# Attention with a gated feed-forward on one core: the first batch in one piece, with two of its head groups paired

## The chip, the cores and the metric

The kernel runs on one core of a Trainium2 chip. The metric is the device time of one execution in microseconds (us). A core has five engines with instruction queues of their own: TensorE (PE in the profile; its weight loads are PEld), VectorE (DVE), ScalarE (ACT), GpSimd (POOL) and SyncE (SP). They meet through semaphores only. Here POOL's queue issues all loads, and SP's (with a few on ACT's) issues all stores.

## The reference, cut to what matters

```python
B, H, S, D = 8, 12, 448, 64          # attention; x has 3584 tokens of 768
scores = q @ k.transpose(0, 1, 3, 2) / sqrt(D)
attn = exp(scores - max) / sum       # softmax over the keys
x = (attn @ v).transpose(0, 2, 1, 3).reshape(B * S, H * D)
h = x @ w_in                         # 768 -> 2048
g = h * (1 / (1 + exp(-h)))          # silu
out = g @ w_out                      # 2048 -> 768
```

## The kernel before, in words

**Head groups and units.** The 12 heads of a batch are taken in three groups of four (HG = 4, NG = 3). A group's q, k and v are loaded for all four heads at once. A *unit* is one group of one batch with a range of query blocks; S = 448 is 14 blocks of 32 (TPP = 14). Batch 0 is cut into two pieces of 7 blocks each (PIECES), so it has six units of 224 queries; every later batch has three units of 448.

**Scores.** `load_k` and `load_q` bring a group's rows into SBUF; `turn_k` and `turn_q` transpose them on VectorE. The keys of a unit lie in four chunks (NCH). `scores` multiplies one chunk with the unit's queries: a matmul uses 32 rows of the array for one head, so four heads can run side by side, and two of them (one `y`) fill one score buffer of two PSUM banks. There are two such buffers (tag "s", bufs=2). For the first HALVES units a burst is cut into halves of two heads each, so that each half has a buffer. `expo` is the exponential on ScalarE, one for each half, 896 elements a partition. In batch 0 of this kernel a burst covers two chunks of 224 queries (`per_burst`), in later batches one chunk of 448.

**Lone and paired units.** A lone unit has chunks of 128, 128, 96 and 96 keys (KROWS). Two paired units ("low" and "high") have three chunks of 128 keys each, and share the fourth, where each has 64: `scores_rest` computes it for both at once. For a pair VectorE adds the first three exponentials of each unit (`add_e`, into T), and `attend_sums` makes both units' softmax sums in three passes over the array; a lone unit needs four for itself. LONES says which units are lone: all of batch 0, and the first group of batch 1.

**Values and norm.** `attend` multiplies exponentials with ones (part 0, the sums) and with the two halves of V (parts 1 and 2), four chunks for each part, four heads side by side in 32 columns of the array. `inverse` turns the sums and takes the reciprocal on VectorE; `norm` scales the products into xT.

**Feed-forward.** `ffn1` makes one block of 128 rows of h out of six passes over xT; `tanh` (ScalarE) and `gate` (VectorE) make silu; `plain` and `product` multiply with w_out. From the second pair of token tiles on, products are taken seven for eight by sums and differences of blocks (`combine_w`, `combine_g`); the last two batches do so in the first layer as well (`pair_product`).

**What sets the order.** A planner (`Order`, lines 82 to 166, and the loop at 1473 to 1525) simulates the engines with costs written into the code and emits the instructions in the order that comes out. Each operation has a busy time and a tail after which its result counts as there; rings stand for buffers. The hardware then runs each engine's queue in exactly that order. Where the planner sees TensorE without work before the first `ffn1`, it emits matmuls with zeros (`run_zeros`), 47 of them at the very start (FIRST). The scores are taken as soon as a buffer is free; values and feed-forward work fill what is left.

**Loads.** All loads stand in POOL's queue in the order of lines 823 to 848. Eight load semaphores go round, so a load's issue waits until the load eight places before it has landed. For batch 0 the order is k and q (first piece) of the three groups, then V of all three groups in four loads, then the second piece's queries between the halves of w_in.

Of the kernel before, what the change touches and what calls it, by code (L numbers as in the profile page):

```python
# [9 lines left out]
FP16 = mybir.dt.float16  # L10
# [7 lines left out]
PE_OUT = 0.20  # L18
HOP = 0.10
DMA_ROW = 0.022  # L20
DMA_RATE = 13570.0
# [60 lines left out]
class Order:  # L82
# [19 lines left out]
    def start(self, op):  # L102
        self.emit(op.emit)
        self.free[op.eng] = self.now + op.busy
        self.busy[op.eng] += op.busy
        op.done = self.now + op.busy + op.tail
        if op.then:
            op.then(op.done)
# [61 lines left out]
def kernel(  # L170
# [29 lines left out]
    PACE = 2.6  # L200
    LONES = (0, 1, 2, 3)
    NPL = 4
    EAGER = 1
    HALVES = 6
    NEAR, LATE = 0.15, -2.0
# [4 lines left out]
    TWB, SXB = 40, 4  # L210
    PIECES = ((0, 7), (7, TPP))
    NE, NX3, NT_ = 9, 6, 2
# [44 lines left out]

    def load_q(n):
        b, hg, g0, g1 = units[n]
        t = sb.tile([128, (g1 - g0) * D], FP16, name=f"rq_{n}", tag="rq", bufs=NRQ)  # L260
        nc.gpsimd.dma_start(out=t, in_=group_of(q, b, hg)[:, D * g0 : D * g1])  # L261
        rawq[n] = t

# [58 lines left out]

    def turn_q(n):
        t = rawq[n][:].bitcast(FP32).rearrange("p (g i) -> p g i", i=32)
        if units[n][0] == B - 1:

            to = sb.tile([128, TPP * D], FP16, name=f"q_{n}", tag="rq", bufs=NRQ)
            nc.vector.transpose(
                out=to[:].bitcast(FP32).rearrange("p (i g) -> p g i", g=TPP), in_=t
            )  # L330
            rawq[n] = to
        else:
            nc.vector.transpose(out=t, in_=t)
        QT[n] = rawq[n].rearrange("p (q e) -> p e q", e=2)
# [7 lines left out]
    def score(pS, n, c, e, h, x0, x1, p0):  # L342
        b, hg, g0, g1 = units[n]
        nq = 32 * (g1 - g0)
        at = nq * (c % per_burst(n))
        nc.tensor.matmul(  # L346
            out=pS[p0 : p0 + 32 * (x1 - x0), h % 2, at : at + nq],
            lhsT=KT[(b, hg)][32 * h : 32 * (h + 1), c, x0:x1, :, e],
            rhs=QT[n][32 * h : 32 * (h + 1), e],
            start=(e == 0),  # L350
            stop=(e == 1),
        )


    def per_burst(n):
        return 2 if units[n][0] == 0 else 1

    def scores(n, w, ys):
        score_banks(n, w, ys)
        for c in range(per_burst(n) * w, per_burst(n) * (w + 1)):  # L360
            for e in range(2):
                for y in ys:
                    for h in (2 * y, 2 * y + 1):
                        score(pS_t[(n, w, y)], n, c, e, h, 0, rows_of(n, c) // 32, 0)


    def scores_rest(n):
        score_banks(n, 3, (0, 1))
        for e in range(2):
            for h in range(HG):  # L370
                pS = pS_t[(n, 3, h // 2)]
                score(pS, n, 3, e, h, 0, 2, 0)
                score(pS, n + 1, 3, e, h, 2, 4, 64)
# [4 lines left out]
    def expo(n, w, y):  # L378
        kr = rows_of(n, w * per_burst(n))
        nk = 32 * (units[n][3] - units[n][2]) * per_burst(n)  # L380
        if (n, w) not in E:
            E[(n, w)] = sb.tile([128, HG, S], FP16, name=f"E_{n}_{w}", tag="E", bufs=NE)
        nc.scalar.activation(  # L383
            out=E[(n, w)][0:kr, 2 * y : 2 * y + 2, 0:nk],
            in_=pS_t[(n, w, y)][0:kr, :, 0:nk],
            func=AF.Exp,
            scale=attn_scale,
        )
# [12 lines left out]
    def attend_mm(a, n, part, c, h, k0, k1, e, start, stop):  # L401
        b, hg, g0, g1 = units[n]
        nq = 32 * (g1 - g0)
        at = nq * (c % per_burst(n))
        if part == 0:
            w = ones[k0:k1, :]
        else:
# [3 lines left out]
            lhsT=w,  # L411
            rhs=e[k0:k1, h, at : at + nq],
            start=start,
# [18 lines left out]

    def attend(ns, part, n):
        if part == 0 and len(ns) == 2:
            attend_sums(ns)
            return
        acc[(n, part)] = ps.tile([128, 512], FP32, name=f"a_{n}_{part}", tag="m", bufs=4)
        for c in range(NCH):
            e = E[(ns[0] if c == NCH - 1 else n, c // per_burst(n))]
            for h in range(HG):  # L440
# [338 lines left out]
    for b in range(B):  # L779
        for g0, g1 in PIECES if b == 0 else ((0, TPP),):  # L780
            units += [(b, hg, g0, g1) for hg in range(NG)]
    NU = len(units)
# [12 lines left out]
    def plan_q(n):  # L795
        g0, g1 = units[n][2:]
        ld_q[n] = od.load(128, 2 * D * (g1 - g0), lambda: load_q(n), rq_ring)

# [22 lines left out]

    NB0 = NG * len(PIECES)
    for hg in range(NG):
        plan_k(0, hg)
        plan_q(hg)
    plan_v(0, 0, NG)
    plan_q(NG)
    plan_q(NG + 1)
    plan_w_in(0, DFF // 2)
    plan_q(NG + 2)  # L830
    plan_k(1, 0)
    plan_q(NB0)
    plan_w_in(DFF // 2, DFF)
    plan_k(1, 1)
    plan_q(NB0 + 1)
    plan_w_out(0, NFF // 4)
    plan_w_out(NFF // 4, NFF // 2)
    plan_k(1, 2)
    plan_q(NB0 + 2)
    for hg in range(NG):  # L840
        plan_v(1, hg, hg + 1)
    plan_w_out(NFF // 2, 3 * NFF // 4)
    plan_w_out(3 * NFF // 4, NFF)
    for n in range(NB0 + NG, NU):
        b, hg = units[n][:2]
# [13 lines left out]
    def plan_turn(n):  # L859
        b, hg, g0, g1 = units[n]  # L860
        if b == B - 1 and not rq_ring.can(1, od.now):
# [10 lines left out]
        if b == B - 1:  # L872
            rq_ring.take()
        qt_op[n] = od.add(
            Op(
                "DVE",
                0.13 + (g1 - g0) / 30.0,
                lambda: turn_q(n),
                [ld_q[n]],
                20,  # L880
                then=rq_ring.give if b == B - 1 else None,
            )
        )
        return True
# [186 lines left out]
    def sums_w(ms):  # L1071

        for m in ms:
# [3 lines left out]
                        "DVE",  # L1077
                        0.9,
                        lambda m=m, f0=f0: combine_w(m, f0, f0 + 4),
# [9 lines left out]
    def queue_plain(t, j):  # L1089
# [6 lines left out]
        def queue(f0, f1):  # L1096
# [17 lines left out]
            def deps():  # L1114
# [3 lines left out]
                for f in range(f0, f1):  # L1118
                    x = g_op.get((0, f), ())
                    if len(x) < len(PIECES):  # L1120
                        return [None]
# [21 lines left out]
    def plan_sums():  # L1143
# [4 lines left out]
        if len(todo) == 4:  # L1148
            gates = {}
            for b in batches(qd):  # L1150
                for f in range(NFF):
                    if len(g_op.get((b, f), ())) < (len(PIECES) if b == 0 else 1):
                        return
# [3 lines left out]
        while todo and (todo[0] == 7 or sg_ring.can(1, od.now)):  # L1157
# [4 lines left out]
            for f0 in (0, 4):  # L1162
                deps = [x for f in range(f0, f0 + 4) for x in gates[f] + gates[f + HF]]
                if m != 5:
# [4 lines left out]
                            "DVE",  # L1169
                            0.34,  # L1170
                            lambda m=m, f0=f0: combine_g(qd, m, f0, f0 + 4),
# [116 lines left out]
    for ns in jobs:  # L1288
        if len(ns) == 1:
            split = ((0,), (1,)) if ns[0] < HALVES else ((0, 1),)  # L1290
            qk_seq += [(ns, c, ys) for c in range(NCH // per_burst(ns[0])) for ys in split]
        else:
            split = ((0,), (1,)) if ns[0] < HALVES else ((0, 1),)
            qk_seq += [([n], c, ys) for n in ns for c in range(NCH - 1) for ys in split]
            qk_seq.append((ns, 3, (0, 1)))
        av_seq += [(ns, 0, ns[0])] + [(ns, part, n) for n in ns for part in (1, 2)]
    pace = {"next": 0.0}
# [18 lines left out]
    def run_qk():  # L1316
# [4 lines left out]
        if ys[0] == 0:  # L1321
# [3 lines left out]
            "PE",  # L1325
            2 * per_burst(n) * mm(nq) + (0.03 if rest else 0.013),
            (lambda: scores_rest(n)) if rest else (lambda: scores(n, c, ys)),
            tail=PE_OUT,
        )
        op.half = len(ys) == 1  # L1330
        if c == NCH // per_burst(n) - 1 and ys[-1] == 1:
            done = []
# [6 lines left out]
        for y in ys:  # L1339
            made = od.add(  # L1340
                Op(
                    "ACT",
                    act(2 * nq * per_burst(n)),
                    lambda y=y: expo(n, c, y),
                    [op],
                    tail=0.2,
                    then=s_ring.give,
# [25 lines left out]
    def av_at():  # L1373
        if not av_seq:
            return None
        ns, part, n = av_seq[0]
        if len(ns) == 2 and part == 0:
# [6 lines left out]
        deps = []  # L1384
        if len(exp_op.get(n, ())) < 2 * NCH // per_burst(n):
            return None
        for i, x in enumerate(exp_op[n]):
            deps.append((x, i // 2 * per_burst(n) * mm(32 * (units[n][3] - units[n][2]))))
        if part:
            deps += [(x, LATE * (units[n][0] == 0)) for x in ld_v[units[n][:2]]]  # L1390
            if units[n][0] > 0:
                deps += [(x, 0.9) for x in rdn_op.get(n, [None])]
        at, m = when(deps), m_ring.when(1)
        return None if at is None or m is None else max(at, m)

    def run_av():
        ns, part, n = av_seq.pop(0)
        b, hg, g0, g1 = units[n]
        nq = 32 * (g1 - g0)
        two = len(ns) == 2  # L1400
        m_ring.take()
        op = Op(
            "PE",
            (3 if two and part == 0 else 4) * mm(nq) + 0.013,
            lambda: attend(ns, part, n),
            tail=PE_OUT,
        )
        if part == 2:

            def then(at):  # L1410
                for _ in range((3 + (n == ns[1])) if two else NCH // per_burst(n)):
                    e_ring.give(at)
# [7 lines left out]
        if part == 0:  # L1420
            after_sums(ns, op, nq)
        else:
            after_av(n, part, op, nq)
# [135 lines left out]
```

## Time and profile before

| what | us |
|---|---|
| median of three timed runs (391.68 to 392.12) | 391.98 |
| the profiled execution, its own time | 392.65 |
| its span, first to last instruction | 390.8 |
| TensorE busy, share of the span | 384.9 (98%) |
| ScalarE busy | 253.8 (65%) |
| VectorE busy | 274.6 (70%) |
| start of the first score matmul | 6.13 |
| start of the first feed-forward matmul | 30.31 |
| zero matmuls, busy | 9.3 (87 of them) |

A row of a timeline gives start and duration, engine, line, operation, output and inputs, shapes and the number of instructions merged; in brackets stands how long the engine was idle before it and what ended that. Durations of single matmuls overlap, so a group's share of time is read from the start of the next row. In the chain of work that ended last, a piece's duration is what it added to the chain. The span's forty slices are 9.77 us each.

### The profile page before, as it was taken

To read this page: it belongs to the slowest core of one execution; us is meant where nothing else is said; L and a number is where in the kernel's file an instruction comes from. 1 tells how busy PE (TensorE), PEld (TensorE's weight loads), DVE (VectorE), ACT (ScalarE), POOL (GpSimd) and SP (SyncE) were. 2 spreads that over 40 slices of the span, in tenths; PEclk is the share of its full clock that TensorE was granted. 3 is DMA by queue.
4 is the path that set the end of the run, shared out by engine and by line. 5 is a ranking of instruction groups with operands and counts; after the bars stand their busy time and mean duration, and the time that the engine had idled before them with its cause. 6 is when DMAs were issued, how large, how long until landed. Compare 5 with 4: busy or idle time off the path is not lost.

```text
span 390.8 us, 10670 instructions
## 1 busy us (share of the span) xinstructions
PE 384.9 (98%) x4369; PEld 206.8 (53%) x4369; DVE 274.6 (70%) x570; ACT 253.8 (65%) x399; POOL 89.1 (23%) x173
## 2 busy tenths in 40 slices
PE   8999999999999999999999999999999999999995
PEld 7657774444444444545445444544445655556663
DVE  2466676999996887887678758666869984447441
ACT  4987885697875779666674766566793338892120
POOL 6632456415006242400643015000000000000000
PEclk9999999999999999999999999999999999999999
DMA  7999999929039582914856129102100131001333
GB/s 116 202 210 210 162 166 180 182 43 142 3 56 148 118 109 37 129 41 93 129 92 89 47 68 164 16 0 54 32 0 3 39 92 33 0 1 38 91 96 102
DMA packets 35330, 34.52 MB, mean 88 GB/s; under 512 B 11345, under 2 KB 33745, under 8 KB 35281
## 3 DMA queue, kind: packets, MB, share of 16 engines
q0 software_dynamic: 24784, 22.82, 39.7%
q1 hardware_dynamic: 10080, 10.53, 9.9%
q8 instruction: 34, 0.56, 0.6%
q10 hardware_dynamic: 416, 0.49, 0.4%
q14 instruction: 16, 0.12, 0.1%
HBM read 45.61 MB, written 11.01 MB: 145 GB/s over the span
## 4 chain that ended last, share of the span: by engine, by line
PE 98%; ACT 1%; issue 0%; DVE 0%
PE p L492 31%; PE h L492 29%; PE s L346 13%; PE a L409 11%; PE f L492 8%; PE o L492 3%; PE z L1468 2%; PE a L425 2%; ACT E L383 1%; ACT ost L768 0%; ACT th L518 0%; DVE zeros L228 0%
## 5 line engine op out<-in xcount | busy, mean ns | idle before, releaser
L383 ACT ACTIVATE E<-s 128x896 f16<-128x896 f32 (+1 forms) x172 | 149.8, 915 | 38.5 <-PE s L346 37.0
L492 PE MATMUL h<-xT,w_in_t 128*32 128x448 f16 (+2 forms) x1086 | 117.1, 336 | 0.0
L492 PEld LDWEIGHTS <-w_in_t 128*128 128x128 f16 (+1 forms) x1158 | 71.1, 97 | 56.3 <-issue 11.5
L518 ACT ACTIVATE th<-h 128x448 f16<-128x448 f32 (+1 forms) x112 | 54.2, 493 | 36.7 <-PE h L492 31.0
L553 DVE SCALAR_TENSOR_TENSOR G<-th,h 128x448 f16<-128x448 f16 (+2 forms) x112 | 55.6, 508 | 23.4 <-ACT th L518 21.7
L492 PEld LDWEIGHTS <-G 128*128 128x128 f16 (+1 forms) x580 | 43.1, 98 | 32.4 <-issue 4.6
L768 ACT COPY ost<-p 128x384 f32<-128x384 f32 x52 | 25.0, 480 | 53.5 <-PE p L492 47.1
L346 PE MATMUL s<-rq,KT 32*128 32x448 f16 (+4 forms) x768 | 51.0, 338 | 0.5 <-ACT E L383 0.4
L280 POOL DMA_DIRECT2D V<-in_v_dram x88 | 48.3, 559 | 13.6 <-DMA w_out_t<-in_moe_w_out_dram 6.5
L492 PE MATMUL p<-w_out_t,G 128*128 128x384 f16 (+1 forms) x352 | 49.5, 326 | 0.0
L409 PE MATMUL a<-E,V 128*32 128x448 f16 (+2 forms) x864 | 42.3, 333 | 0.0
L492 PEld LDWEIGHTS <-S 128*128 128x128 f16 (+1 forms) x408 | 30.0, 98 | 22.7 <-issue 2.3
L261 POOL DMA_DIRECT2D rq<-in_q_dram x27 | 15.1, 558 | 103.9 <-PE s L346 83.1
L492 PE MATMUL p<-D,S 128*128 128x384 f16 (+1 forms) x256 | 37.1, 326 | 0.0
L480 DVE SCALAR_TENSOR_TENSOR xT<-a,rdn 128x448 f16<-128x448 f32 (+1 forms) x54 | 30.4, 568 | 6.4 <-PE a L409 4.4
L774 DVE TENSOR_TENSOR ost<-p,ost 128x384 f32<-128x384 f32 x39 | 21.6, 554 | 18.7 <-PE p L492 13.6
L346 PEld LDWEIGHTS <-KT 32*128 32x128 f16 (+2 forms) x864 | 17.5, 99 | 28.9 <-issue 27.6
L409 PEld LDWEIGHTS <-V 128*32 128x32 f16 (+1 forms) x864 | 20.5, 96 | 18.8 <-issue 7.6
L394 DVE TENSOR_TENSOR T<-E,E 128x1792 f16<-128x1792 f16 x20 | 21.7, 1083 | 8.1 <-ACT E L383 7.9
L394 DVE TENSOR_TENSOR T<-T,E 128x1792 f16<-128x1792 f16 x20 | 21.7, 1083 | 5.7 <-ACT E L383 5.7
L315 DVE STREAM_TRANSPOSE KT<-rk 128x256 f32<-128x256 f32 (+3 forms) x48 | 16.6, 384 | 7.2 <-DMA rk<-in_k_dram 6.4
L492 PE MATMUL p<-w_out_t,S 128*128 128x384 f16 (+1 forms) x152 | 19.1, 326 | 0.0
(67 smaller groups left out, 321.9 us busy)
## 6 DMA issues: line engine op xcount, KB each, us to landing
out_dram<-ost SPq DMA_DIRECT2D x194, 48.0 KB, 1.6
rk<-in_k_dram POOLq DMA_DIRECT2D x24, 224.0 KB, 5.6
rq<-in_q_dram POOLq DMA_DIRECT2D x21, 224.0 KB, 5.8
w_in_t<-in_moe_w_in_dram POOLq DMA_DIRECT2D x6, 512.0 KB, 11.1
w_out_t<-in_moe_w_out_dram POOLq DMA_DIRECT2D x4, 768.0 KB, 13.5
V<-in_v_dram POOLq DMA_DIRECT2D x43, 64.0 KB, 3.9
V<-in_v_dram POOLq DMA_DIRECT2D x40, 48.0 KB, 4.2
rq<-in_q_dram POOLq DMA_DIRECT2D x6, 112.0 KB, 6.1
```

Of the source, the lines that this page charges most:

```text
L280: nc.gpsimd.dma_start(out=VT[b][32 * x : 32 * (x + 1), hs, 0:count, :], in_=v[b, hs].rearrange("h (i g) d -> i h g d", g=TPP)[:, :, first ...
L315: nc.vector.transpose(out=pairs[:, x:y, 0:count], in_=t[:, first : first + count * (y - x)].rearrange("p (x c) i -> p x c i", c=count),)
L346: nc.tensor.matmul(out=pS[p0 : p0 + 32 * (x1 - x0), h % 2, at : at + nq], lhsT=KT[(b, hg)][32 * h : 32 * (h + 1), c, x0:x1, :, e], rhs=QT[ ...
L383: nc.scalar.activation(out=E[(n, w)][0:kr, 2 * y : 2 * y + 2, 0:nk], in_=pS_t[(n, w, y)][0:kr, :, 0:nk], func=AF.Exp, scale=attn_scale,)
L394: nc.vector.tensor_tensor(out=T[n], in0=T[n] if step else E[(n, 0)], in1=E[(n, step + 1)], op=ALU.add,)
L409: nc.tensor.matmul(out=a[32 * h : 32 * (h + 1), 0:nq], lhsT=w, rhs=e[k0:k1, h, at : at + nq], start=start, stop=stop,)
L480: nc.vector.scalar_tensor_tensor(out=x3(b, cc)[:, cc % 3, 32 * g0 : 32 * g1], in0=acc[(n, part)][:, 0:nq], scalar=0.5, in1=rdn_t[n].rearra ...
L492: nc.tensor.matmul(out=out[i : i + cut], lhsT=w[:, i : i + cut], rhs=x, start=start, stop=stop, skip_group_check=True,)
L518: nc.scalar.activation(out=th, in_=h_t[(b, f, t0)][:, 0 : t1 - t0], func=AF.Tanh)
L553: nc.vector.scalar_tensor_tensor(out=dst[:, f, at + lo : at + hi], in0=th_t[(b, f, t0)][:, lo - t0 : hi - t0], scalar=1.0, in1=h_t[(b, f, ...
L768: nc.scalar.copy(out=ost(qd, *OUT[m]), in_=bank(qd, BANK[m]))
L774: nc.vector.tensor_tensor(out=t, in0=bank(qd, BANK[m]), in1=t, op=ALU.add)
```

## The change

Batch 0 is no longer cut into two pieces: its three groups are three units of 448 queries, and `per_burst` goes. Its first two groups become a pair; LONES keeps the third group and the first of batch 1. HALVES is 3, which is still all of batch 0; the shared last chunk of a split pair comes in two halves too (`scores_rest` with `ys`). For unit 0 the value products of the first three chunks are queued ahead of the pair's sums, and the last chunk after them (`attend` with `c0`, `c1`). V of batch 0 is loaded by head group, four loads each, the first two groups ahead of k and q of the third. The queries of unit 0 are loaded and turned in two halves of 7 blocks (`pieces`). The planner's costs change: ScalarE and VectorE count as free 0.09 and 0.07 us before an operation's end (OVERLAP), the exponential's tail is 0.06 instead of 0.2, and two VectorE costs are raised a little.

```diff
+OVERLAP = {"ACT": 0.09, "DVE": 0.07}
...
-        self.free[op.eng] = self.now + op.busy
+        self.free[op.eng] = self.now + op.busy - OVERLAP.get(op.eng, 0.0)
...
-    LONES = (0, 1, 2, 3)
+    LONES = (2, 3)
...
-    HALVES = 6
+    HALVES = 3
...
-    PIECES = ((0, 7), (7, TPP))
...
+    def pieces(n):
+        return ((0, TPP // 2), (TPP // 2, TPP)) if n == 0 else ((0, TPP),)
+
+    def load_q(n, g0, g1):
+        b, hg = units[n][:2]
+        if g0 == 0:
+            rawq[n] = sb.tile([128, TPP * D], FP16, name=f"rq_{n}", tag="rq", bufs=NRQ)
+        cols = slice(D * g0, D * g1)
+        nc.gpsimd.dma_start(out=rawq[n][:, cols], in_=group_of(q, b, hg)[:, cols])
...
-    def per_burst(n):
-        return 2 if units[n][0] == 0 else 1
...
-    def scores_rest(n):
-        score_banks(n, 3, (0, 1))
+    def scores(n, c, ys):
+        score_banks(n, c, ys)
         for e in range(2):
-            for h in range(HG):
+            for y in ys:
+                for h in (2 * y, 2 * y + 1):
+                    score(pS_t[(n, c, y)], n, c, e, h, 0, rows_of(n, c) // 32, 0)
+
+
+    def scores_rest(n, ys):
+        score_banks(n, 3, ys)
+        for e in range(2):
+            for h in range(2 * ys[0], 2 * ys[-1] + 2):
...
-    def attend(ns, part, n):
+    def attend(ns, part, n, c0, c1):
...
-        for c in range(NCH):
-            e = E[(ns[0] if c == NCH - 1 else n, c // per_burst(n))]
+        for c in range(c0, c1):
+            e = E[(ns[0] if c == NCH - 1 else n, c)]
...
-    for hg in range(NG):
+    for hg in range(2):
         plan_k(0, hg)
         plan_q(hg)
-    plan_v(0, 0, NG)
+    for hg in range(2):
+        plan_v(0, hg, hg + 1)
+    plan_k(0, 2)
+    plan_q(2)
+    plan_w_in(0, DFF // 2)
+    plan_v(0, 2, 3)
+    plan_k(1, 0)
     plan_q(NG)
-    plan_q(NG + 1)
-    plan_w_in(0, DFF // 2)
-    plan_q(NG + 2)
-    plan_k(1, 0)
-    plan_q(NB0)
     plan_w_in(DFF // 2, DFF)
...
+        for (g0, g1), load in zip(pieces(n), ld_q[n]):
+            qt_op[n] = od.add(
...
+                    lambda g0=g0, g1=g1: turn_q(n, g0, g1),
+                    [load] + ([qt_op[n]] if g0 else []),
...
-                        0.9,
+                        0.95,
...
-                            0.34,
+                            0.40,
...
-            qk_seq.append((ns, 3, (0, 1)))
-        av_seq += [(ns, 0, ns[0])] + [(ns, part, n) for n in ns for part in (1, 2)]
+            qk_seq += [(ns, 3, ys) for ys in split]
+        whole = [(ns, part, n, 0, NCH) for n in ns for part in (1, 2)]
+        if ns[0] == 0:
+            av_seq += [(ns, part, 0, 0, NCH - 1) for part in (1, 2)]
+            whole[:2] = [(ns, part, 0, NCH - 1, NCH) for part in (1, 2)]
+        av_seq += [(ns, 0, ns[0], 0, NCH)] + whole
...
-                    tail=0.2,
+                    tail=0.06,
```

## The prediction

> **What bounds the kernel now.** First the page's busy shares, its slices and its chain, to see which engine sets the end:
>
> ```profile
> PE 384.9 (98%) x4369; PEld 206.8 (53%) x4369; DVE 274.6 (70%) x570; ACT 253.8 (65%) x399; POOL 89.1 (23%) x173
> ...
> PE   8999999999999999999999999999999999999995
> ...
> PEclk9999999999999999999999999999999999999999
> ...
> PE 98%; ACT 1%; issue 0%; DVE 0%
> ```
>
> TensorE is busy everywhere at full granted clock, and the chain is its own queue. Next its list of waits, which shows what else it ever waited for:
>
> ```profile
> PE z L1468 <- DVE zeros L228: 1.0, 1, 1.0
> PE a L409 <- issue: 0.5, 1, 0.5
> PE s L346 <- ACT E L383: 0.4, 1, 0.4
> ```
>
> That is all: 1.9 us. So the time is TensorE's instructions, added up. But "busy" counts the zero matmuls (L1468), so the third view is TensorE's timeline of the opening (start, us, what):
>
> ```profile
> 1.00 5.19 PE L1468 MATMUL z<-zeros 128*128 128x128 f16 x47 [1.00 <-DVE zeros L228]
> 6.13 0.70 PE L346 MATMUL s<-rq,KT 32*128 32x224 f16 x16
> 6.76 0.62 PE L1468 MATMUL z<-zeros 128*128 128x128 f16 x8
> 7.83 0.60 PE L346 MATMUL s<-rq,KT 32*96 32x224 f16 x8 [0.44 <-ACT E L383]
> 8.36 0.28 PE L1468 MATMUL z<-zeros 128*128 128x128 f16 x2
> 8.63 0.60 PE L346 MATMUL s<-rq,KT 32*96 32x224 f16 x8
> ...
> 30.31 0.75 PE L492 MATMUL h<-xT,w_in_t 128*128 128x224 f16 x6
> ```
>
> Up to 16 us a half burst of scores comes every 0.8 to 1 us with zeros between: the exponentials pace it. From 30.31 the feed-forward fills everything. Last, the chain in order of time gives the price of one step:
>
> ```profile
> 41.05 2.41 PE h L492 x24
> ...
> 191.37 2.38 PE h L492 x12
> 193.75 0.51 PE s L346 x8
> ...
> 241.94 17.14 PE h L492 x90
> ```
>
> 17.14 us for 90 gives 0.189 us for a 448-column pass. Twelve of them are 2.27, so 0.11 of the 2.38 belongs to changing between the feed-forward's and the scores' shape of tile; the burst (two passes, 0.38) leaves 0.13. I take 0.12 a change. The 224-column pass is (2.41 - 0.11) / 24 = 0.096. From the two, a 128-column zero is 0.056; the first 47 took 5.19, 0.110 each.
>
> **The change, part by part.** The sum is made against the profiled execution (392.65 us, span 390.8); the median shown, 391.98, lies 0.67 below it.
>
> Passes of batch 0. Scores: 24 half bursts of 4 x 0.096 become 22 of 2 x 0.189 (the pair shares its last chunk): 9.21 to 8.33, -0.88. Sums and values: 72 passes of 224 columns become 31 of 448 (3 + 16 for the pair, 12 for the lone group): 6.91 to 5.87, -1.04. First feed-forward layer: 192 passes to 96, 18.42 to 18.17, -0.25. Together -2.17.
>
> Changes of tile shape. Counted in the two built orders there are 207 before (49 ahead of the first h pass) and 196 after (42 ahead of it): -11 x 0.12 = -1.32. A change of shape drains TensorE, says the Trainium skill (TensorEngine Tiling (Array Packing), Key Properties), and TensorE: Matmul & The Clock Gate (Step-by-step) puts a drain at some 128 cycles; 128 / 2.4 GHz is an estimate of 0.053 us. By it this term would be -0.58 and the time 0.74 us above mine. The rows, 0.11 and 0.13, are dearer than that, so I keep 0.12.
>
> Zeros. 47 + 40 become 51 + 50: 4 x 0.110 + 10 x 0.056 = +1.00. They stand in the order and run whether or not anyone waits.
>
> Early value passes. Three of the four chunks of unit 0's two value products move ahead of the pair's sums, between half bursts of unit 1. The work is the same; the first needs V's first head group.
>
> First queries. Before, the first score needs k and half the queries of hg 0: they land at 4.86 and 5.34 (issued 1.26 and 1.94, 3.6 and 3.4 to landing), the turn follows, the score starts at 6.13, 0.65 after the turn's DVE was free at 5.48. Now every score streams all 448 queries, so it needs both halves, and the second is the third load. Fast end: 112 KB behind q took 0.48 behind k, so 5.82. Slow end: the third load of before, k of hg 1, landed at 2.48 + 5.8 = 8.28. It had twice the bytes; half of its 2.94 behind q gives 6.81, which I take. Score at 6.81 + 0.65 = 7.46. TensorE gets there at 1.00 + 51 x 0.110 + 0.12 = 6.75: idle +0.7 (ends 0 and 2.2). All of TensorE's queue stands behind it.
>
> Exponentials. The page's 0.44 wait at 7.83 goes: -0.44. ScalarE's first five ran 4.17 us, (4.17 - 0.915) / 4 = 0.815 apart. The new order puts two or three zeros between half bursts: 0.38 + 2 x 0.12 + 0.11 or 0.17, 0.73 or 0.79. Eight bursts ahead of the early values are thus each 0.03 to 0.08 too soon: +0.45 (ends 0, where work between hides it, and 1.0, all 13 of the pair's).
>
> Hidden, at nothing: four adds of 1.083 (T, L394) on VectorE, which in 10 to 20 us is busy 4.64 of 10; the last stands behind exponential 12 and ahead of the pair's sums, which leaves three half bursts as cover: 2.4 us less the exponential's own 0.9. If that is gone, up to 1.08. On POOL two more q and k issues fall away with the second piece, V's four become twelve at 0.55 each plus two 0.31 memsets. POOL holds eight loads in flight (before, its 11th issue waited for the third load's landing), so k and q of hg 2 now stand behind eight V pieces. By bytes they are there in time: 1835 KB through q of hg 2, where before had 1720 landed at 14.3 and 1950 at 15.3; wanted at about 18. V's first group, 1147 KB, lies between 10.9 and 11.7; wanted at 13.6. The planner's new constants (OVERLAP, tail 0.06) reorder the rest of the program; TensorE has no wait there and queued feed-forward work is the cover, so nothing, bounds -0.5 (the 0.5 "issue" gap goes) and +1.
>
> Sum: -2.17 - 1.32 + 1.00 + 0.7 - 0.44 + 0.45 = -1.78. Profiled 390.9; on the median 390.2.
>
> **Rivals.** *Late queries of batch 1 (slower).* In the built order the first score of (1, 0) stands behind 51 + 44 zeros, 22 half bursts, 27 passes and some 41 changes: 1.00 + 5.63 + 2.46 + 8.34 + 5.11 + 4.92 = 27.5, plus 1.15 of the waits above, 28.6; before it came at 30.99. Its q must land 0.9 (turn 0.62, start 0.28) sooner, at 27.7. By bytes it lands as before's did, since the same 4095 KB go first: 16.64 + 9.2 = 25.8. But through eight slots: the first w_in load waits for the eighth load (a V piece, 5.45 + 7.7 = 13.1), lands 10 later at 23.1 and only then lets q go, and 9.2 more is 32.3. TensorE would stand 4.6 us: 394.8. It turns the sign from a landing at 30.3. For it: V pieces keep few bytes in flight. Against: eight are still some 450 KB, and those latencies were measured behind full queues. The Trainium skill speaks for this rival: DMA: Bandwidth & Descriptors (Rules for kernel authors) says to coalesce small transfers, as under 64 KB one pays mostly overhead. In this trace V's 64 KB pieces took a median of 3.9 us to land and k's 224 KB ones 5.6, which bears it out in part.
>
> *Second half of q as late as k was (no change).* At 8.28 idle is 2.2, not 0.7: 391.7. For it: DMA moves only 108 to 131 GB/s from 5 to 6.5 us. Against: half the bytes.
>
> *Nothing waits (better).* The half lands at 5.82 and the exponentials keep up: 390.2 - 0.7 - 0.45 = 389.0. Against: the two-zero bursts are shorter than 0.815.
>
> **How the numbers follow.** Forecast 0.58, own range 389.5 to 391.1; late queries 0.16; late half 0.15; nothing waits 0.11. Within 0.2% (0.8 us, about what a measurement of this kernel can tell) of 391.98 counts as same. Faster 0.58 + 0.11, a little of the forecast's tail going to same: 0.68. Same 0.16. Slower 0.16. Range 389.0 to 392.0: it takes in the late half and the better case and leaves out the late queries.
>
> **What would show it.** Right: TensorE's last product ends near 385.2 (before 386.9); first score at 7.2 to 7.7 behind a DVE wait; first h pass near 30; waits on ACT E some 0.4 to 0.8 in all, each under 0.1. Wrong: a wait on DMA or DVE rq ahead of the scores at 13, 19 or 28 us; a wait of the value passes on V near 13; new waits behind 60 us, where I claim none; an idle before the first score above 1.5.

## The result, and the profile after

The kernel after the change took 393.59 us in the median of 22 executions (391.58 to 398.65), the kernel before 392.07 in 22 run beside it. The ratio is 1.0038, 95% interval 1.0024 to 1.0052: slower, where 390.2 and faster was forecast, and outside the range. Ratios, here and below, leave out the executions more than 1.5% above the fastest of their kernel (here two of the 22); medians are of all. The executions of the kernel after spread over 7 us, those of the kernel before over 0.8 (391.65 to 392.49). They go mostly with the clock that TensorE was granted, as a mean over the execution: 391.6 to 392.3 us at 0.999 and 1.0, 393.2 to 395.0 from 0.985 to 0.990, 396.1 to 398.7 under 0.98. The order is not strict (391.75 at 0.991, 394.69 at 0.996).

The profiled execution took 394.69 us, 2.04 more than the one of before. The page of the kernel after: busy shares, two of the forty-slice rows, and the summary of the chain.

```profile
PE 382.6 (97%) x4279; PEld 190.9 (49%) x4279; DVE 272.2 (69%) x539; ACT 249.1 (63%) x381; POOL 92.5 (24%) x181
...
PE   6988999999999999999999999999999999999996
...
PEclk9998999999999999999999999999999999999999
...
PE 89%; DMA 8%; POOL 1%; DVE 1%; issue 1%; ACT 0%; DVEq 0%; POOLq 0%
```

TensorE has 2.3 us less work than before (384.9), as the count of passes promised, and the program is longer. The loss lies in the first four slices, up to 39 us: TensorE is idle there, the clock drops in the fourth, and 8% of the chain are now transfers. TensorE's list of waits (total, times, longest):

```profile
PE s L348 <- DVE rq L337: 3.6, 2, 1.9
PE a L406 <- DMA V<-in_v_dram: 1.1, 1, 1.1
PE z L1480 <- DVE zeros L228: 1.0, 1, 1.0
PE s L348 <- ACT E L381: 0.6, 1, 0.6
```

Its timeline shows where they stand (start, us, what; the idle before it in brackets):

```profile
1.00 4.48 PE L1480 MATMUL z<-zeros 128*128 128x128 f16 x51 [1.00 <-DVE zeros L228]
7.25 0.58 PE L348 MATMUL s<-rq,KT 32*128 32x448 f16 x8 [1.76 <-DVE rq L337]
7.76 0.51 PE L1480 MATMUL z<-zeros 128*128 128x128 f16 x6
8.82 0.57 PE L348 MATMUL s<-rq,KT 32*128 32x448 f16 x4 [0.55 <-ACT E L381]
...
28.72 0.94 PE L406 MATMUL a<-E,V 128*32 128x448 f16 x16 [1.05 <-DMA V<-in_v_dram]
31.54 0.93 PE L348 MATMUL s<-rq,KT 32*128 32x448 f16 x8 [1.88 <-DVE rq L337]
32.40 1.68 PE L406 MATMUL a<-E,V 128*32 128x448 f16 x16
...
34.63 1.40 PE L492 MATMUL h<-xT,w_in_t 128*128 128x448 f16 x6
```

Two things are to be seen. TensorE stands at 28 and at 31 us, first for V of the third head group and then for the queries of batch 1, which landed at 28.7 and 30.8. And the row at 32.40 takes 1.68 for the same 16 matmuls that took 0.94 at 28.72: they ran at half speed. The windows of the same trace say so too (window, its length, busy time and number of TensorE's instructions, of the other engines, then the granted clock, the DMA engines' share and GB/s):

```profile
31.50:34.50 3.00, 2.96 (x29) 1.08 (x30) 2.38 (x5) 1.73 (x2) 1.38 (x3) 0.50 1.05 135
34.50:35.00 0.50, 0.50 (x6) 0.36 (x4) 0.26 (x1) 0.00 (x0) 0.00 (x0) 0.68 1.03 168
```

In this execution the clock thus held through the early idle of 1.76 (the score burst at 8.82 takes 0.57; at half speed the same burst takes 0.93 in the run below) and fell behind the late one. Behind 35 us TensorE waits for nothing. The chain up to there, in order of time, tells how the queries came late:

```profile
3.52 6.52 DMA rq<-in_q_dram
...
10.32 0.54 POOL V L284
10.87 0.54 POOL rk L255
11.41 0.53 POOL rq L266
11.94 9.47 DMA w_in_t<-in_moe_w_in_dram
...
21.70 9.12 DMA rq<-in_q_dram
...
30.83 0.66 DVE rq L337
```

POOL cannot issue its last V piece of the second group before the second group's queries have landed (issued at 3.52, eight loads earlier), nor k, q and w_in behind it; the queries of batch 1 wait for the first w_in load, and take 9 more. The bytes came more slowly than before as well. The same stretch, 10 to 20 us, in windows of before and then of after:

```profile
10.00:20.00 10.00, 10.00 (x191) 6.57 (x191) 4.64 (x13) 9.41 (x12) 5.93 (x10) 1.00 1.25 203
```

```profile
10.00:20.00 10.00, 9.98 (x114) 3.73 (x111) 6.25 (x8) 9.72 (x13) 6.47 (x11) 1.00 0.93 125
```

203 GB/s against 125, in a stretch in which POOL issues five pieces of V of 32 to 64 KB, where before had issued its V in four loads of up to 192 KB. That the size of the pieces made the difference was not tried. V of the third group was not held back at POOL: its four pieces were issued from 14.03 to 15.90 and took 12.7 to 13.7 us to land, behind the three w_in loads of 512 KB each that begin at 11.94.

### The profile page after: what moved, and what is told of

The parts are those of the page before. It is cut to its first block, busy times and chain, and to the rows that moved or that the text cites. A ratio compares the mean times of both kernels' runs of the same rounds, so it can differ in the third digit from the quotient of the medians.

```text
span 392.9 us, 10438 instructions
## 1 busy us (share of the span) xinstructions
PE 382.6 (97%) x4279; PEld 190.9 (49%) x4279; DVE 272.2 (69%) x539; ACT 249.1 (63%) x381; POOL 92.5 (24%) x181
## 4 chain that ended last, share of the span: by engine, by line
PE 89%; DMA 8%; POOL 1%; DVE 1%; issue 1%; ACT 0%; DVEq 0%; POOLq 0%
PE p L492 29%; PE h L492 29%; PE s L348 9%; PE a L406 9%; PE f L492 8%; DMA rq<-in_q_dram 5%; PE o L492 3%; DMA w_in_t<-in_moe_w_in_dram 2%; PE a L422 2%; POOL rk L255 0%; POOL rq L266 0%; DVE rq L337 0%; PE z L1480 0%; DVE sT L450 0%; POOL V L284 0%
## 5 line engine op out<-in xcount | busy, mean ns | idle before, releaser
L381 ACT ACTIVATE E<-s 128x896 f16<-128x896 f32 (+1 forms) x170 | 146.2, 916 | 37.4 <-PE s L348 36.8
L492 PE MATMUL h<-xT,w_in_t 128*32 128x448 f16 (+1 forms) x1206 | 116.7, 353 | 0.0
L492 PEld LDWEIGHTS <-w_in_t 128*32 128x32 f16 (+1 forms) x1278 | 63.0, 97 | 62.7 <-issue 10.7
L518 ACT ACTIVATE th<-h 128x448 f16<-128x448 f32 x96 | 52.4, 546 | 37.6 <-PE h L492 33.9
L553 DVE SCALAR_TENSOR_TENSOR G<-th,h 128x448 f16<-128x448 f16 (+1 forms) x96 | 53.7, 567 | 22.3 <-ACT th L518 21.4
L284 POOL DMA_DIRECT2D V<-in_v_dram x96 | 52.3, 552 | 20.3 <-DMA w_out_t<-in_moe_w_out_dram 6.1
L348 PE MATMUL s<-rq,KT 32*128 32x448 f16 (+2 forms) x672 | 48.9, 364 | 4.3 <-DVE rq L337 3.6
L406 PE MATMUL a<-E,V 128*32 128x448 f16 (+1 forms) x768 | 42.2, 358 | 1.2 <-DMA V<-in_v_dram 1.1
L480 DVE SCALAR_TENSOR_TENSOR xT<-a,rdn 128x448 f16<-128x448 f32 x48 | 28.5, 615 | 3.5 <-PE a L406 2.3
L348 PEld LDWEIGHTS <-KT 32*128 32x128 f16 (+2 forms) x768 | 12.7, 97 | 33.7 <-issue 27.8
## 6 DMA issues: line engine op xcount, KB each, us to landing
w_in_t<-in_moe_w_in_dram POOLq DMA_DIRECT2D x6, 512.0 KB, 10.2
```

The source lines that it names most:

```text
L284: nc.gpsimd.dma_start(out=VT[b][32 * x : 32 * (x + 1), hs, 0:count, :], in_=v[b, hs].rearrange("h (i g) d -> i h g d", g=TPP)[:, :, first ...
L348: nc.tensor.matmul(out=pS[p0 : p0 + 32 * (x1 - x0), h % 2, 0 : 32 * (g1 - g0)], lhsT=KT[(b, hg)][32 * h : 32 * (h + 1), c, x0:x1, :, e], r ...
L381: nc.scalar.activation(out=E[(n, w)][0:kr, 2 * y : 2 * y + 2, 0:nk], in_=pS_t[(n, w, y)][0:kr, :, 0:nk], func=AF.Exp, scale=attn_scale,)
L406: nc.tensor.matmul(out=a[32 * h : 32 * (h + 1), 0:nq], lhsT=w, rhs=e[k0:k1, h, 0:nq], start=start, stop=stop,)
L480: nc.vector.scalar_tensor_tensor(out=x3(b, cc)[:, cc % 3, 32 * g0 : 32 * g1], in0=acc[(n, part)][:, 0:nq], scalar=0.5, in1=rdn_t[n].rearra ...
L492: nc.tensor.matmul(out=out[i : i + cut], lhsT=w[:, i : i + cut], rhs=x, start=start, stop=stop, skip_group_check=True,)
```

## Experiments

No kernel here leaves out any of the computation: they move loads, zero matmuls and value passes, or undo one part of the change. Two theories stood against each other. One says that the loads alone did it: put them in time and the forecast holds. The other says that the idle time itself costs more than it lasts, because the clock falls behind it.

**The loads in another order.** V of the third group, and k and q of batch 1, are issued ahead of w_in's first half.

```diff
     plan_k(0, 2)
     plan_q(2)
-    plan_w_in(0, DFF // 2)
     plan_v(0, 2, 3)
     plan_k(1, 0)
     plan_q(NG)
+    plan_w_in(0, DFF // 2)
```

> The changed kernel with one edit: V of head group 2 and k and q of batch 1's first group are loaded ahead of the first half of w_in, not behind it. Theory 'late loads' (the loss is the 1.05 us wait for V and the 1.88 us wait for the turned q of batch 1 at 28 to 31 us, and the half clock of 31.5 to 34.8 us that follows this idle): both waits go, and with them some 1.6 us of half clock; about 4.5 us off 393.6, so 389 to 390, if w_in, now last, still lands before the first h pass at about 29; if it does not, 1 to 2 us of that come back as a wait of h on w_in. Rival 'plan' (the new planner costs leave waits all over the program): no change, 393 to 394.

Measured: 395.04 us (390.8 to 399.01, 12 executions), ratio 1.0057 (1.0029 to 1.0084). The waits at 28 and 31 are gone; 1.2 ahead of the first score is left:

```profile
PE s L348 <- DVE rq L337: 1.2, 1, 1.2
...
PE s L348 <- ACT E L381: 0.6, 1, 0.6
```

And yet it is no faster than the kernel after. In this execution the clock was down from 9 to 19 us, behind that first wait and the 0.55 for the exponential (columns as above):

```profile
6.00:9.00 3.00, 1.25 (x20) 0.69 (x19) 0.99 (x4) 1.01 (x2) 2.15 (x6) 1.00 1.18 190
9.00:14.00 5.00, 5.00 (x28) 1.30 (x29) 1.93 (x3) 3.87 (x5) 4.45 (x9) 0.50 1.03 133
14.00:19.00 5.00, 5.00 (x43) 1.15 (x43) 2.23 (x4) 3.06 (x4) 4.07 (x7) 0.50 1.14 172
```

The one execution of the twelve at clock 1.0 took 390.8; those at 0.986 some 393.3 to 394.1, the one at 0.969 took 399.01. 389 to 390 was expected: a miss. The edit moves the loads and leaves V's pieces as small as they were, the third group's now land after about 5 us instead of 13, and the late waits go; so the place in the queue was enough. The clock is what is left.

**Zeros into the late idle.** The loads stay as changed; 18 zeros go ahead of the value products that waited for V, and 32 ahead of the scores that waited for q.

```diff
+        if n == NG and c == 0 and 0 in ys:
+            run_zeros(32)
         score_banks(n, c, ys)
...
+        if n == 2 and part == 1:
+            run_zeros(18)
         if c0 == 0:
```

> The changed kernel with 18 more zero matmuls ahead of head group 2's first value product and 32 more ahead of the first score of batch 1, to fill the two idle stretches (1.05 and 1.88 us) without moving anything else. Theory 'clock' (the idle lets the granted clock fall to 0.5 for 3.3 us, worth about 1.6 us, and is why executions differ by up to 7 us): 391.5 to 392.3, granted clock 1.00 at 31 to 35 us, and executions within 1.5 us of each other. Rival (the clock falls but nothing waits for TensorE there, or it falls for another reason): 393 to 394 and the same spread.

Measured: 399.55 (395.31 to 400.43, 6 executions), ratio 1.0174 (1.0141 to 1.0208). A miss. The clock was 0.50 from 10.2 to 27.2 us here, behind an early idle of no more than 0.65; the late idle was filled, but this edit does not touch what stands ahead of 10 us.

**Zeros into the early idle.** Nothing but 24 more zeros at the very start, 75 instead of 51. In the kernel after, TensorE idled there from 5.5 to 7.25, so these zeros stand in time that was idle.

```diff
             warm["z"] = ps.tile([128, 512], FP32, name="z", tag="m", bufs=4)
+            n += 24
```

> The changed kernel with 24 more zero matmuls at the very start, the rest of the order untouched. Theory 'clock in the opening' (the gap between the first zeros and the first score lets the granted clock fall to 0.5 at 9 to 10 us, in most executions, and under half bursts it takes 10 to 20 us to come back): the gap is filled, the clock stays at 1.00 until the wait at 28 us, executions lie within 1.5 us of each other and the median at 391.5 to 392.5. Rival (the clock falls for another reason, as in the executions of the second round of kernels): the same spread of 7 us and a median of 393 or more; the zeros would then cost up to 0.7 us more.

Measured: 392.06 (391.26 to 396.71, 12 executions), ratio 1.0011 (0.9987 to 1.0036): 1.5 us less than the kernel after, for 24 instructions more. Eight of the twelve ran at clock 0.999 or 1.0. The executions were expected within 1.5 us of each other, and spread over 5.5. The first score starts where it did (7.29 against 7.25). The queries of batch 1 are still late in the profiled execution (turned at 29.41, against 30.83), and without a fall of the clock they cost just the wait:

```profile
PE s L348 <- DVE rq L337: 1.6, 1, 1.6
...
PE s L348 <- ACT E L381: 0.6, 1, 0.6
```

**Both edits**, the loads and the 24 zeros.

> Both edits: V of head group 2 and k and q of batch 1's first group ahead of w_in, and 24 more zeros at the start. If the loss has two causes, the clock and the late loads, and no third: 390 to 391, clock 1.00 throughout, no wait of TensorE above 0.7 us behind 9 us, and a narrow spread. If a third cause is left (the planner's costs, the pair): 391.5 or more.

Measured: 390.65 (390.06 to 391.86, 6 executions), ratio 0.996 (0.9947 to 0.9973): faster than before. Against the zeros alone the loads bring 1.4 us, near the 1.6 of that wait. The waits left:

```profile
PE z L1481 <- DVE zeros L228: 1.0, 1, 1.0
PE s L348 <- ACT E L381: 0.5, 1, 0.5
```

That is the list of before again, but for its gap of 0.5, with the smaller work of the change. The profiled execution is the slowest of the six (391.86): its clock was at half from 11.3 to 18.1 us, with no idle ahead of the first score and the 0.55 alone behind it.

**The early idle in the kernel before.** If an idle ahead of the first score costs the clock whatever the change, it must do so in the kernel before. There 21 of the first 47 zeros are left out.

```diff
             warm["z"] = ps.tile([128, 512], FP32, name="z", tag="m", bufs=4)
+            n -= 21
```

> The kernel before with 21 of its first 47 zero matmuls left out and nothing else, so that TensorE stands some 2 us ahead of its first score. Theory 'clock in the opening': the first zeros keep the clock up, so now it is at half through much of the opening: 3 to 6 us slower than 392.2, with a spread of several us. Rival (a gap ahead of the first score costs nothing by itself, the change's other parts do): 392 as before.

Measured: 407.88 (407.63 to 408.58, 5 executions), ratio 1.0402 (1.0389 to 1.0415). Its timeline:

```profile
1.00 2.96 PE L1469 MATMUL z<-zeros 128*128 128x128 f16 x26 [1.00 <-DVE zeros L228]
5.98 0.96 PE L346 MATMUL s<-rq,KT 32*128 32x224 f16 x16 [2.03 <-DVE rq L333]
6.88 1.03 PE L1469 MATMUL z<-zeros 128*128 128x128 f16 x8
...
44.85 1.30 PE L492 MATMUL h<-xT,w_in_t 128*128 128x224 f16 x6
```

The first score starts where it did (5.98 against 6.13), but takes 0.96 instead of 0.70, the eight zeros behind it 1.03 instead of 0.62, and the first feed-forward pass comes at 44.85 instead of 30.31. From 6 to some 46 us everything ran at half speed with TensorE busy throughout, and the time is 15.7 us longer, where 3 to 6 was expected. The 26 zeros took 0.114 each, so the clock was low from the start and had not come up when the idle began. The run changes two things at once, the idle and the number of zeros, and does not tell which of them kept the clock down. The page's row of the granted clock reads full speed there: where no change of the clock is recorded, durations have to be read instead. Three of the 94 executions of the untouched kernel before, at 406 to 408 us, have the same time.

**The clock over all executions.** Mean granted clock under 0.997, for each kernel of this section and those below:

| kernel | first zeros | executions | of them under 0.997 | median of all | median of the rest |
|---|---|---|---|---|---|
| after | 51 | 22 | 20 | 393.59 | 391.94 |
| loads in another order | 51 | 12 | 11 | 395.04 | 390.80 |
| zeros into the late idle | 51 | 6 | 6 | 399.55 | none |
| first queries whole | 51 | 10 | 8 | 394.12 | 391.77 |
| late values | 51 | 4 | 4 | 396.83 | none |
| 24 zeros | 75 | 12 | 4 | 392.06 | 391.80 |
| 24 zeros, loads (both) | 75 | 6 | 1 | 390.65 | 390.62 |
| both, old planner costs | 75 | 12 | 0 | 392.29 | 392.29 |
| both, late values | 75 | 12 | 2 | 391.15 | 391.06 |
| both, no pair | 75 | 12 | 3 | 392.85 | 392.80 |
| both, ten zeros in the gap | 75 | 5 | 0 | 390.43 | 390.43 |
| both, first queries whole | 75 | 12 | 1 | 391.50 | 391.48 |

With 51 first zeros 49 of 54 executions lost clock, with 75 it was 11 of 71. The last column is, as far as the record of the clock shows it, what each order of work costs when the clock stays up. Kernels with 51 and with 75 first zeros were not run side by side, but the kernel before was run beside all of them, and its medians (392.07, 392.25, 392.27 and 392.13) moved by no more than 0.2.

That the 24 zeros mostly hold the clock up is shown by these counts. That it is the idle which brings it down is not, for the zeros also lengthen the run of work ahead of the first score. The traced executions do not sort by the idle (the slow zeros are estimated from the total of the first zeros, at 0.110 for a slow and 0.056 for a fast one):

| kernel | first zeros, us | of them slow, fast | idle ahead of the first score | clock behind it |
|---|---|---|---|---|
| before | 5.19 | 47, 0 | none | held |
| after | 4.48 | 30, 21 | 1.76 | held to 31.5 |
| first queries whole | 4.28 | 26, 25 | 1.84 | held to 31 |
| late values | 5.08 | 41, 10 | 1.80 | half from 9 |
| loads in another order | 5.17 | 43, 8 | 1.20 | half from 9 |
| zeros into the late idle | 5.62 | 51, 0 | 0.65 | half from 10.2 |
| 24 zeros | 6.36 | 40, 35 | none | held |
| both | 6.05 | 34, 41 | none | half from 11.3 |
| both, old planner costs | 6.93 | 51, 24 | 0.42 | held |
| both, late values | 5.76 | 29, 46 | 0.35 | held |
| both, no pair | 6.67 | 46, 29 | none | held |
| both, ten zeros in the gap | 5.88 | 31, 44 | 1.54 | held |
| both, first queries whole | 5.76 | 29, 46 | 0.83 | held |

Of the four longest idles in this table only one was followed by a fall. With an idle ahead of the first score the clock fell where 10 zeros or fewer had run fast before it, and held where 21 or more had. One trace of each kernel is few, and no run was made to test this.

**The parts of the change, one by one.** First, with the loads as changed, the first queries in one piece:

```diff
-        return ((0, TPP // 2), (TPP // 2, TPP)) if n == 0 else ((0, TPP),)
+        return ((0, TPP),)
```

> The changed kernel with the first queries loaded and turned in one piece. Theory 'two halves gain little': the one load of 224 KB lands within 0.3 us of the second half, its turn takes 0.62 instead of 0.41, the first score starts 0 to 0.5 us later, and since TensorE waits for loads at 28 us anyway the time stays at 393 to 394. Rival (the halves cost: the additional load takes one of the eight slots and delays every load behind it): 0.5 us or more faster.

Measured: 394.12 (10 executions), ratio 1.0046 (1.0019 to 1.0074), like the kernel after; the first score came at 7.13, no later than with halves. Next, unit 0's values whole and behind the sums again:

```diff
-        if ns[0] == 0:
-            av_seq += [(ns, part, 0, 0, NCH - 1) for part in (1, 2)]
-            whole[:2] = [(ns, part, 0, NCH - 1, NCH) for part in (1, 2)]
```

> The changed kernel with unit 0's value products whole and behind the pair's sums, as the other units have them. Theory 'late loads': whatever this moves in the opening is taken up by the waits at 28 to 31 us, so 393 to 394, and the first score of batch 1 starts within 0.3 us of 31.5. Rival 'TensorE's own work paces the opening': the value passes come out of the gaps between exponentials and cost their 1.1 us again: 394.5 or more.

Measured: 396.83 (4 executions), ratio 1.0119 (1.0103 to 1.0134). In all four the clock was down (0.50 from 9 to 20 us, 0.54 to 30 in the profiled one), so this run doesn't tell what the early values are worth. Both parts were therefore undone again on the kernel with both edits, where the clock mostly holds. Of the five runs on it, the four behind the first were made in a later session, in which the kernel before took 392.13 against 392.27, so differences of 0.1 to 0.2 against the 390.65 say nothing. The planner's old costs on that kernel:

```diff
-OVERLAP = {"ACT": 0.09, "DVE": 0.07}
+OVERLAP = {}
...
-                    tail=0.06,
+                    tail=0.2,
```

> The same as the kernel with both edits, but with the planner's costs of before (nothing free early, the exponential's tail 0.2, the two VectorE costs as they were). If the new costs are worth what the sum of the prediction gave them (nothing but the zeros and waits of the opening), this has more zeros between the half bursts and is 0 to 0.8 us slower than it. If the new costs bring new waits behind the opening, it is faster.

Measured: 392.29 (12 executions), ratio 0.9999 (0.999 to 1.0008), 1.6 us more than with the new costs. More than the 0 to 0.8 that was expected. The two kernels' groups of zeros, with the new costs and then with the old ones, point to a reason:

```profile
L1481 PE MATMUL z<-zeros 128*128 128x128 f16 x122 | 11.7, 251 | 1.0 <-DVE zeros L228 1.0
```

```profile
L1481 PE MATMUL z<-zeros 128*128 128x128 f16 x142 | 13.5, 253 | 1.0 <-DVE zeros L228 1.0
```

A planner that takes the exponential for longer puts 20 more zeros ahead of the first feed-forward pass (20 x 0.056 = 1.1), and three more changes of shape (44 against 41, 0.36), and TensorE runs them whether or not it had to wait. By count that is 1.5 of the 1.6. The traces bear out a part only: from the first score to the first feed-forward pass the old costs took 23.41 us, against 22.78 to 23.10 in three of the runs below at full clock, so 0.3 to 0.6. The rest is open; in this profiled execution the first score also came late, at 8.35 against 7.16.

The values behind the sums, on the kernel with both edits:

> The kernel with both edits (loads in the other order, 24 more zeros at the start), whose five undisturbed times lay at 390.06 to 390.83, with unit 0's value products put back whole behind the pair's sums. The passes of TensorE are the same and the zeros 124 instead of 122, +0.11. Theory: the early values are worth what they cover. Between half bursts that come every 0.815 they stand in for nothing but zeros, and six passes with four changes (1.13 + 0.48) would have to be done later: up to +1.6 if the half bursts are paced by the exponentials all the same. Expected 391.2 (390.6 to 392.2). Rival: they are worth nothing, because the planner puts other work there: 390.5. A third reading, that the late values themselves brought on the fall of the granted clock in the earlier run without them (396.8, clock 0.50 from 9 to 30 us): then the clock falls here too, and the time is 394 or more.

Measured: 391.15 (12 executions), ratio 0.9987 (0.9964 to 1.001). The early values are worth 0.4 to 0.5 us at full clock, under the 0.5 to 1.6 that they were thought to cover; two of twelve executions lost clock, so late values by themselves do not bring on the fall.

No pair in batch 0, on the kernel with both edits:

```diff
-    LONES = (2, 3)
+    LONES = (0, 1, 2, 3)
```

> The kernel with both edits, and all three groups of batch 0 lone as before the change (no pair). It adds two half bursts of scores (4 passes) and five passes of sums, 9 x 0.189 = 1.70, five zeros (0.28) and some changes of shape (0.2 to 0.5); two more exponentials for ScalarE at 0.815, which pace the opening. By the prediction's way of counting: +2.0 to +2.5, 392.5. Rival: the exponentials, not TensorE, set the opening, so that the passes of the sums hide and only the two exponentials count: +1.6, or less, 391.5 to 392.

Measured: 392.85 (12 executions), ratio 1.0036 (1.0015 to 1.0058). The pair is worth 2.2 us, as counted by passes, zeros and changes (2.0 to 2.5). Without it the kernel with both edits would be slower than before.

Ten zeros in the idle of 0.55 behind the first exponential, on the kernel with both edits:

```diff
+        if n == 0 and c == 1 and 0 in ys:
+            run_zeros(10)
         score_banks(n, c, ys)
```

> The kernel with both edits, and ten more zeros (0.56) in the idle of 0.55 behind the first exponential, which is now the last idle of the opening. Theory: the fall of the granted clock at 9 to 11 us, which was left in one of six executions of the kernel with both edits, comes from that idle; so no execution shows a clock below 0.995, and since the zeros fill time that was idle anyway, the median is 390.3 to 390.6. Rival: the fall comes from something else (the chip, or the whole level of work in the opening); then one execution in six still falls, to about 392.

Measured: 390.43 (390.28 to 391.41, 5 executions), ratio 0.9961 (0.9949 to 0.9974), as fast as without the zeros (390.65, ratio 0.996). None of five lost clock, but with one of six before that settles nothing. In its profiled execution the first queries were turned late, TensorE idled 1.54 ahead of the first score at 8.42, and the clock held all the same.

The first queries whole, on the kernel with both edits:

> The kernel with both edits, and the first queries loaded and turned in one piece. In the kernel after without any other edit the first score came at 7.25 with halves and at 7.13 with one piece, so the halves should be worth nothing: 390.3 to 390.8, no wait ahead of the first score behind the longer zeros. Rival: the halves are worth the half turn (0.3) at the first score: 390.9.

Measured: 391.5 (390.67 to 395.91, 12 executions), ratio 0.9991 (0.997 to 1.0011). Nothing was expected of the halves; the medians differ by 0.8. In the profiled execution, one of the two fastest (390.69), the first score waited 0.83 and started at 7.60, 0.44 later than with halves, and the time was the same as with halves. Where the 0.8 comes from is thus not shown; that the slower ones had a later landing was not seen, since they have no trace.

## Why the prediction was wrong, point by point

**Passes and changes of shape, -2.17 and -1.32: right as far as tested.** TensorE's busy time fell by 2.3 although zeros were added. With the two causes below taken away the kernel takes 390.65, which is 1.6 under the kernel before run beside it (392.27), against -1.78 forecast, and undoing the pair costs 2.2 by the same way of counting. A sum that comes out says little of its terms one by one, and those below did not all hold. The 0.12 for a change of shape was never measured alone; the row that it rests on, 17.14 for 90, gives 0.190 for a pass and not 0.189, and with it 0.10 for a change where 0.11 was read. That moves the sum by less than 0.1.

**Zeros, +1.00: mis-sized.** The first 51 were taken at 0.110 each, 5.6 in all, because before's 47 ran so. Here they took 4.48: with 0.110 for a slow and 0.056 for a fast one, 30 were slow and 21 fast. TensorE was done at 5.5.

**First queries, idle +0.7: the start was right; the clock behind it, put at nothing, is a step that failed.** The first score was put at 7.46 and came at 7.25, the half landing at 6.8 where 6.81 was taken. The idle ahead of it was 1.76, above the 1.5 named as a sign of error, because the zeros ended early. In time that cancels. The sum took "full granted clock" from the view of before, held it for the kernel after, and so put the clock at nothing; it was under 0.997 in 20 of 22 executions. (Nor was it full in the kernel before, whose first 47 zeros took 0.110 each.) The run with nothing but 24 more zeros, which leaves the starts as they are, prices this: 393.59 - 392.06 = 1.5 us, or 1.7 against the kernel before run beside each. Whether those zeros help by filling the idle or by a longer run of work is open.

**Exponentials, -0.44 and +0.45: right in sum, by luck.** The wait of 0.44 that was to go became one of 0.55 at another place, so this part is +0.1. The eight small waits that were to make up for it do not show as waits; the half bursts stand 0.81 apart, as the spacing of the exponentials has it.

**"By bytes it lands as before's did": this step failed too.** It stood against the rival of the late queries and put the queries of batch 1 at 25.8. They landed at 30.8. (The same way of counting held for k and q of the third group, "by bytes they are there in time": q was turned at 16.68, wanted at about 18.) The rival's chain came as written, through the eight loads in flight: w_in issued at 11.94 (13.1 forecast), landed at 21.41 (23.1), then q for 9.12 (9.2). It was put at 0.16 since eight loads are still many bytes; the trace shows 125 GB/s where before had 203. V of the third group, which no step named, was late as well, behind the bytes of w_in. The score of batch 1 was wanted at 28.6, rightly: 31.54 less the waits of 1.05 and 1.88 is 28.61. Price in the profiled execution: 1.05 + 1.88 of waits, and some 1.65 of the half speed behind them (3.3 us at 0.50). In the median, with 24 more zeros: 392.06 - 390.65 = 1.4. The rival's own price, 4.6 of waiting, was too high, and the late loads without the fall of the clock only take the gain away (392.06, before 392.27): they do not make the change slower. The Trainium skill's rule quoted there (DMA: Bandwidth & Descriptors, Rules for kernel authors), to coalesce small transfers, was not tried: the runs show that the order of the loads was enough.

**The planner's costs, nothing behind 60 us: right there.** No wait appears in the kernel after, and before's gap of 0.5, put at nothing with a bound of -0.5, is gone. The new costs are worth 1.6, by the count of zeros in part, which the prediction took from the built order without putting it down to the costs.

From the forecast to the result: 390.2, 0.45 unexplained (0.3 of it is the kernel before, 391.98 then and 392.27 beside that run), 1.4 for the late loads, 1.5 for the clock make 393.6. The two prices hold for this order of undoing only. Taking away the late loads first showed no gain (395.04): the clock alone made a larger loss than both together, with 5 of 12 executions under 0.98 against 5 of 22. Why is open. So it is the clock that turned the sign, and the late loads that took the gain once the clock was held.

## What to carry to other kernels

When TensorE is the bound, the opening is not priced by its work and its waits alone: look at what the clock does, read from the duration of one kind of matmul, over many executions. Zeros in an idle that is there anyway delayed nothing here, and they were worth more than most of the parts of the change. And where loads stand in one queue with a fixed number in flight, follow the chain of landings piece by piece; the sum of bytes leaves out which load waits for which, and here it was 5 us off.

## What the runs showed of the hardware that was not expected

- **The clock falls without a long idle, and in some executions only.** In the traces it fell to 0.50 behind idles of 1.80, 1.20, 0.65 and none ahead of the first score, each with one of 0.55 a half burst later, and it held behind 1.84, 1.76 and 1.54. With 51 first zeros it was under 0.997 in 49 of 54 executions, with 75 in 11 of 71. The Trainium skill (TensorE: Matmul & The Clock Gate, What's actually happening) has the slow clock follow at least one idle window of about 3.4 us and full speed after about 3.4 us of sustained work, by a window that runs free of the kernel. A free window would fit that the same order of work falls in one execution and not in the next; no run here shows the window itself, and no idle here was as long as 3.4.
- **Recovery can be slow under this work.** The clock stayed at half for 7 us (both edits), 10 (loads), 17 (zeros into the late idle), some 20 (late values), and in the kernel before with 21 zeros fewer from its first matmul to 46 us, with TensorE busy from 6 on. Behind the late idle of the kernel after it was 3.3 (31.5 to 34.8), which agrees with the 3.4 us of sustained work that the Trainium skill gives (TensorE: Matmul & The Clock Gate, What's actually happening); the longer ones do not. What in the opening's mix of score bursts, zeros and value passes keeps it down was not tried.
- **The warm-up at the start varies.** Estimated as above from the total of the first zeros: 2.9 to 3.4 us slow in five traces, 3.8 with both edits, 5.6 with the old costs, and all 5.19 in the kernel before. The 3.4 that the Trainium skill gives (TensorE: Matmul & The Clock Gate, What's actually happening) is near the low end.
- **The record of the granted clock has a blind start.** It reads 1.00 until the first change is recorded, over zeros of 0.110 and, in the kernel before with fewer zeros, over 40 us of half speed. A mean near 1.0 is thus no proof of full clock; none of the executions at 0.997 or more in the table, though, was over 2 us above the fastest of its kernel.
